# Two of a head's four casts on GpSimd instead of ScalarE, and its cluster rows sent with the first cast

## The chip, the core and the metric
The kernel runs on one core of a Trainium2 chip. Its engines work side by side, each through its own list of instructions in order: TensorE (PE; its weight loads are shown apart as PEld), VectorE (DVE), ScalarE (ACT), GpSimd (POOL) and SyncE (SP), which issues nearly all DMA transfers. The metric is the device time of one execution in microseconds (us), lower is better.

## The reference
The program is a chain of three stages; only the first is touched by the change. It is attention for 2 batches of 8 heads, sequence 768, head size 64, in which a query sees only the keys of its own cluster:

```
q_assign = argmax(einsum('bhsd,hcd->bhsc', q_n, c_n))     # 16 centroids a head
k_assign = argmax(einsum('bhsd,hcd->bhsc', k_n, c_n))
mask = q_assign[:, :, :, None] == k_assign[:, :, None, :]
scores = where(mask, q @ k.T / sqrt(64), -1e9)
attn = softmax(scores) @ v
```

Its output, 1536 rows of 512, goes through a mixture of 8 experts (each row to one expert, two matrix products with a ReLU), and then through a dense pair of products with a softplus between them.

## The kernel before, in words
**Tiles and order.** There are 16 heads, two to a pair p. A head has NT = 6 tiles of 128 queries, so the attention loop has 96 steps g = 6h + t. All engines' instructions are written out in this loop by hand, in program order; each engine works through its own in that order and waits by semaphores. In step g TensorE computes S, the scores, of tile g + 2, turns P of tile g (`P_T`, into the bank Tp), and does one piece of the product with v of the head before (`AV`). VectorE takes the row maximum `nm` of S, ScalarE the exponential P. The turned tile goes from Tp to PT in two halves: by VectorE and ScalarE, or both by ScalarE in steps listed in `busy`.

**Operands of S.** The products run in float32 with operands split into a rounded part and a rest. A head has four operand tiles, from a pool with two buffers of each: kA holds the rounded k in one half of the partitions and again in the other half, qA the rounded q and its rest, qB the rounded q, kB the rest of k. `prep_part(h, i)` makes them in four parts i = 0 to 3 at steps g = 6(h - 2) + 3 + i, so two heads ahead. Partitions 64 to 79 of qB and kB hold the one-hot cluster rows of queries and keys, by which the second product of S (L319) adds the mask. They are made for a pair at once in `mks[p]` (16 x 4 rows), and `put_mask(h)` copies them by four DMA transfers on SyncE's queue. L304, the first product of S, reads qA and kA; L319 reads qB and kB.

**Assignment of clusters.** `sims_mm`, `sims_T`, five small steps `sims_max` and `sims_back` make `mks[p]` during the pair before; for pairs from 3 on the third step, `eq` (L202), is on GpSimd, and the next, a maximum (L203), on VectorE. All transposes of this kind share one PSUM bank, misc.

**Other work in the loop.** `load_raw(p)` reloads q and k of a pair at step 12p - 25, once the old pair's are read. 16 pieces of the dense stage's weights come as 64-bit words (`cv_load`, 128 x 1024 x 8 bytes), are turned into float32 by ScalarE (`cvd`, L451) and VectorE (L453, L454, L459, L463), and are stored by SyncE (L469, w_rows).

The step's end, where the parts and the rows are called (before the change):

```
h2, i2 = divmod(g - 3, NT)
h2 += 2
if 2 <= h2 < NH and i2 < 4:
    prep_part(h2, i2)
    if i2 == 3 and h2 > 2:
        put_mask(h2)
```

Of the kernel before, what the change touches and what calls it, by code (L numbers as in the profile page):

```python
# [13 lines left out]
AF = mybir.ActivationFunctionType  # L14
ALU = mybir.AluOpType
# [17 lines left out]
def body(ctx, tc, qT, kT, vP, cen, mod, wg, bias, w1, w2, win, wout, out):  # L33
# [13 lines left out]
    pe, dve, act, pool, sp = nc.tensor, nc.vector, nc.scalar, nc.gpsimd, nc.sync  # L47
# [107 lines left out]
    def drain():  # L155
        while pend:
            for _ in pend.pop(0):
                pass

    def run(f, *a):  # L160

        drain()
        x = f(*a)
        if hasattr(x, "__next__"):
            next(x, None)
            pend.append(x)
# [101 lines left out]
    def prep_part(h, i):  # L268

        p, o = h // 2, 64 * (h % 2)  # L270
        if i == 0:
            spl[h] = tuple(p_sp.tile([128, S], F32R, tag=n, name=n) for n in ("qA", "kA", "qB", "kB"))
        qA, kA, qB, kB = spl[h]
        q_s, k_s = (r[o:o + 64] for r in raw[p])
        hi, lo = slice(o, o + 64), slice(64 - o, 128 - o)
        if i == 0:
            act.copy(kA[hi], k_s)
        elif i == 1:
            act.copy(kA[lo], k_s)
            dve.tensor_tensor(out=kB[0:64], in0=k_s, in1=kA[hi].bitcast(F32), op=ALU.subtract)  # L280
        elif i == 2:
            act.activation(out=qA[hi], in_=q_s, func=AF.Copy, scale=0.125)
        else:
            act.activation(out=qB[0:64], in_=q_s, func=AF.Copy, scale=0.125)
            dve.scalar_tensor_tensor(
                out=qA[lo], in0=q_s, scalar=0.125, in1=qA[hi].bitcast(F32), op0=ALU.mult, op1=ALU.subtract
            )

    def put_mask(h):
        p, i = h // 2, h % 2  # L290
        qA, kA, qB, kB = spl[h]
        for j, x in enumerate((qB, kB)):
            for a in range(2):
                o = 64 * j + 32 * a + 16 * i
                sp.dma_start(
                    out=x[64:80, a * HS:(a + 1) * HS].bitcast(F32), in_=mks[p][o:o + 16].bitcast(F32)
                )
# [11 lines left out]
    def S_mm(g):  # L309
        if g >= NH * NT:  # L310
            return
        if g not in S_t:
            S_part(g)
        h, t = divmod(g, NT)
        qA, kA, qB, kB = spl[h]
        ps = S_t[g]
        ts = slice(t * 128, t * 128 + 128)
        for i in range(2):
            pe.matmul(ps[:, i, :HS], qB[:80, ts], kB[:80, i * HS:(i + 1) * HS], start=False, stop=True)  # L319
        nm_t[g] = p_m.tile([128, 1], F32, tag="nm", name="nm", bufs=4)  # L320
        dve.tensor_reduce(out=nm_t[g], in_=ps[:, :, :HS], axis=AX.XY, op=ALU.max, negate=True)  # L321

    def S_exp(g):
        if g >= NH * NT:
            return
        h, t = divmod(g, NT)
        if t == 0:
            sums[h] = p_m.tile([128, NT], F32, tag="sums", name="sums", bufs=3)
        P_t[g] = p_P.tile([128, 2, HS], F32, tag="P", name="P")
        act.activation(  # L330
            out=P_t[g], in_=S_t.pop(g)[:, :, :HS], func=AF.Exp, bias=nm_t.pop(g), scale=1.0,
            accum_out=sums[h][:, t:t + 1],
        )

    def P_T(g):
        h, t = divmod(g, NT)
        if t == 0:
            PT[h] = p_PT.tile([128, NT, S], F32, tag="PT", name="PT")
        P = P_t.pop(g)
        for i in range(2):  # L340
            ps = ps_T.tile([128, 3, 128], F32, tag="t", name="Tp")
            for j in range(3):
                pe.transpose(ps[:, j, :], P[:, i, j * 128:(j + 1) * 128], ident)  # L343
            dst = PT[h][:, 3 * i:3 * i + 3, t * 128:(t + 1) * 128]
            if i == 0 and g not in busy:
                dve.tensor_copy(dst, ps)
            else:
                act.copy(dst, ps)  # L348
# [20 lines left out]
    def av_step(g):  # L369

        h, kt = divmod(g - NT - 1, NT)
        if kt == NT - 1:
            return
        AV(h, kt)
        if kt == NT - 2:
            AV(h, NT - 1)
            fin_av(h)
# [566 lines left out]
    with tc.manual_schedule():  # L944
# [147 lines left out]
        for g in range(NH * NT):  # L1092
            h, t = divmod(g, NT)
            if g > NT:
                av_step(g)
            S_mm(g + 2)
            P_T(g)
            for f, a in jobs.get(g, ()):
                if inspect.isgeneratorfunction(f):
                    run(f, *a)  # L1100
                else:
                    f(*a)
            S_exp(g + 2)
            drain()
            for f, a in after.get(g, ()):
                f(*a)
            h2, i2 = divmod(g - 3, NT)
            h2 += 2
            if 2 <= h2 < NH and i2 < 4:
                prep_part(h2, i2)  # L1110
                if i2 == 3 and h2 > 2:
                    put_mask(h2)
            if g == 8:
                put_mask(2)
# [450 lines left out]
        for c, y in enumerate((ys[NM - 1][1], ps_A.tile([128, 512], F32, tag="a", name="o"))):  # L1565
            cs = slice(c * 256, c * 256 + 256)
            for kt in range(16):
                gh, gl = gs[NM - 1, kt // 4]
                hi, lo = wts["out", kt // 2]
# [51 lines left out]
```

## Time and profile before

| what | value |
|---|---|
| median of 3 runs | 767.64 us (766.39 to 768.34) |
| the profiled execution, its own time | 767.36 us |
| its span in the profile | 765.6 us |
| busy in the span: TensorE, VectorE, ScalarE, GpSimd | 708.8, 450.0, 416.1, 128.5 us |

The span runs from the first to the last instruction in the profile; the execution's own time has 1.8 us more around it. Busy time is an average over stages that differ: attention ends near 297 us, the experts follow, and then the dense stage. "Granted clock" is the share of TensorE's full clock, of 2.4 GHz, that it was given in a stretch; the other level is 1.2 GHz. "Waited for" names what came last before an instruction could start.

### The profile page before, as it was taken

What the parts mean: (1) busy time and instruction counts of PE and PEld (TensorE: products, weight loads), DVE (VectorE), ACT (ScalarE), POOL (GpSimd) and SP (SyncE); (2) the same over time, 40 slices, a digit from 0 to 9 for tenths busy, and PEclk for the clock granted to TensorE, in tenths of its full rate; (3) what the DMA queues carried; (4) which work ended last, traced back from release to release, by engine and by line L of the source; (5) the groups of instructions that cost most, each with busy time, mean ns of one, the idle gap of its engine ahead of it and who ended that gap; (6) DMA issues with size and microseconds to landing.
All of it is one profiled execution on the core that took longest, in us unless ns stands there. A gap on an engine that the chain in (4) does not pass through costs nothing. (4 is left out here: it accounts for less than half of the span.)

```text
span 765.6 us, 11692 instructions
## 1 busy us (share of the span) xinstructions
PE 708.8 (93%) x4498; PEld 564.4 (74%) x4498; DVE 450.0 (59%) x668; ACT 416.1 (54%) x663; POOL 128.5 (17%) x144
## 2 busy tenths in 40 slices
PE   4997997899798999986999999998999999999998
PEld 2764654556455555874879888997998898999887
DVE  5895987789789975863446563677143233233220
ACT  3886987798779976343446562663323323323310
POOL 4200000000310103635452522252000000000000
PEclk9898999999989999996999999999999999999999
DMA  4314454544553625979967985500010000000000
GB/s 133 105 56 174 145 198 151 171 145 160 183 131 119 199 98 167 236 110 368 355 228 277 345 301 195 179 15 20 10 42 15 28 15 15 15 1 28 1 28 27
DMA packets 38683, 99.28 MB, mean 130 GB/s; under 512 B 8255, under 2 KB 15615, under 8 KB 36577
## 3 DMA queue, kind: packets, MB, share of 16 engines
q1 hardware_dynamic: 35888, 91.42, 36.3%
q0 software_dynamic: 2592, 6.69, 2.4%
q8 instruction: 36, 0.59, 0.3%
q10 hardware_dynamic: 144, 0.39, 0.2%
q14 instruction: 23, 0.18, 0.1%
HBM read 79.13 MB, written 18.28 MB: 127 GB/s over the span
## 5 line engine op out<-in xcount | busy, mean ns | idle before, releaser
L1500 DVE SCALAR_TENSOR_TENSOR sp<-g,sp 128x1024 f32<-128x1024 f32 x24 | 29.4, 1224 | 148.8 <-ACT sp L1499 148.8
L321 DVE TENSOR_REDUCE nm<-S 128x1 f32<-128x768 f32 x96 | 90.9, 948 | 34.3 <-PE S L319 34.0
L1489 PE MATMUL g<-xh,wh 128*128 128x256 f32 x384 | 108.7, 283 | 0.0
L1489 PE MATMUL g<-xh,wl 128*128 128x256 f32 x384 | 107.9, 281 | 0.0
L1489 PE MATMUL g<-xl,wh 128*128 128x256 f32 x384 | 107.9, 281 | 0.0
L1497 ACT ACTIVATE sp<-g 128x1024 f32<-128x1024 f32 x24 | 24.6, 1027 | 136.6 <-PE g L1489 126.7
L330 ACT ACTIVATE P<-S,nm 128x768 f32<-128x768 f32 x96 | 86.9, 905 | 18.9 <-DVE nm L321 16.2
L343 PE MATMUL Tp<-ident,P 128*128 128x128 f32 x576 | 85.6, 284 | 10.7 <-ACT PT L348 7.5
L343 PEld LDWEIGHTS Tp<-ident,P 128*128 128x128 f32 x576 | 68.7, 144 | 24.5 <-ACT PT L348 14.2
L355 PE MATMUL av<-PT,v 128*64 128x384 f32 x384 | 80.7, 517 | 0.0
L741 POOL TENSOR_TENSOR wl<-raw,wh 128x1024 fp32r<-128x1024 f32 x22 | 54.1, 2469 | 139.2 <-ACT wh L740 132.2
L741 DVE TENSOR_TENSOR wl<-raw,wh 128x1024 fp32r<-128x1024 f32 x50 | 65.1, 1343 | 14.5 <-ACT wh L740 14.5
L1489 PEld LDWEIGHTS g<-xl,wh 128*128 128x128 f32 x384 | 73.0, 190 | 0.5
L740 ACT CAST wh<-raw 128x1024 fp32r<-128x1024 f32 x69 | 68.9, 1050 | 8.0 <-DMA raw<-in_w 5.4
L1489 PEld LDWEIGHTS g<-xh,wh 128*128 128x128 f32 x384 | 72.8, 190 | 0.5
L348 ACT COPY PT<-Tp 128x384 f32<-128x384 f32 x144 | 64.0, 477 | 16.8 <-PE Tp L343 16.0
L1489 PEld LDWEIGHTS g<-xh,wl 128*128 128x128 f32 x384 | 73.0, 190 | 0.0
L1524 PE MATMUL o<-wh,gT 128*128 128x512 f32 x216 | 69.7, 394 | 0.0
L319 PE MATMUL S<-kB,qB 80*128 80x384 f32 x192 | 51.8, 353 | 18.0 <-DMA kB<-mk 16.1
L843 PE MATMUL y<-wh,hT 128*128 128x512 f32 x192 | 64.7, 408 | 0.0
L304 PEld LDWEIGHTS S<-kA,qA 128*128 128x128 f32 x192 | 29.7, 194 | 47.1 <-ACT PT L348 16.2
L304 PE MATMUL S<-kA,qA 128*128 128x384 f32 x192 | 60.2, 396 | 1.2 <-ACT P L330 0.9
(284 smaller groups left out, 1396.9 us busy)
## 6 DMA issues: line engine op xcount, KB each, us to landing
raw<-in_w SPq DMA_DIRECT2D x56, 512.0 KB, 7.6
words<-in_win SPq DMA_DIRECT2D x8, 1024.0 KB, 7.4
w_rows<-cvt SPq DMA_DIRECT2D x16, 512.0 KB, 3.0
words<-in_wout SPq DMA_DIRECT2D x8, 1024.0 KB, 5.7
whole<-in_w SPq DMA_DIRECT2D x16, 512.0 KB, 6.2
raw<-w_rows SPq DMA_DIRECT2D x16, 512.0 KB, 4.6
rawq<-in_qT SPq DMA_DIRECT2D x8, 384.0 KB, 3.4
v<-in_vP SPq DMA_DIRECT2D x8, 384.0 KB, 3.4
```

What stands on the lines that cost most here:

```text
L304: pe.matmul(ps[:, i, :HS], qA[:, t * 128:t * 128 + 128], kA[:, i * HS:(i + 1) * HS], start=True, stop=False)
L319: pe.matmul(ps[:, i, :HS], qB[:80, ts], kB[:80, i * HS:(i + 1) * HS], start=False, stop=True)
L321: dve.tensor_reduce(out=nm_t[g], in_=ps[:, :, :HS], axis=AX.XY, op=ALU.max, negate=True)
L330: act.activation(out=P_t[g], in_=S_t.pop(g)[:, :, :HS], func=AF.Exp, bias=nm_t.pop(g), scale=1.0, accum_out=sums[h][:, t:t + 1],)
L343: pe.transpose(ps[:, j, :], P[:, i, j * 128:(j + 1) * 128], ident)
L348: act.copy(dst, ps)
L355: pe.matmul(av_t[h][64 * a:64 * a + 64, :], vt[p][:, kt, 64 * i:64 * i + 64], PT[h][:, kt, a * HS:(a + 1) * HS], start=(kt == 0), stop=(kt ...
L740: cp(self.hi, self.raw)
L741: eng.tensor_tensor(out=self.lo, in0=self.raw, in1=self.hi.bitcast(F32), op=ALU.subtract)
L843: pe.matmul(u["y"][j], x, y, start=(kt == 0 and i == 0), stop=(kt == 7 and i == 2))
L1489: pe.matmul(o, a, b[:, kt, :], start=(n == 0 and f % 2 == 0), stop=(n == 11), skip_group_check=True)
L1524: pe.matmul(ys[u][j], x[:, a:a + 128], y, start=(kt == 0 and i == 0), stop=(kt == 15 and i == 2))
```

## The change
Two of a head's four casts, the second copy of the rounded k (part 1) and qB (part 3), go from ScalarE to GpSimd, where they stand in parts 0 and 2. The cluster rows are sent in part 0 instead of part 3, for heads from 3 on.

```diff
@@ -275,13 +275,13 @@
         if i == 0:
             act.copy(kA[hi], k_s)
+            pool.tensor_scalar(out=kA[lo], in0=k_s, scalar1=1.0, scalar2=1.0, op0=ALU.mult, op1=ALU.mult)
         elif i == 1:
-            act.copy(kA[lo], k_s)
             dve.tensor_tensor(out=kB[0:64], in0=k_s, in1=kA[hi].bitcast(F32), op=ALU.subtract)
         elif i == 2:
             act.activation(out=qA[hi], in_=q_s, func=AF.Copy, scale=0.125)
+            pool.tensor_scalar(out=qB[0:64], in0=q_s, scalar1=0.125, scalar2=1.0, op0=ALU.mult, op1=ALU.mult)
         else:
-            act.activation(out=qB[0:64], in_=q_s, func=AF.Copy, scale=0.125)
             dve.scalar_tensor_tensor(
                 out=qA[lo], in0=q_s, scalar=0.125, in1=qA[hi].bitcast(F32), op0=ALU.mult, op1=ALU.subtract
             )
@@ -1108,7 +1108,7 @@
             if 2 <= h2 < NH and i2 < 4:
                 prep_part(h2, i2)
-                if i2 == 3 and h2 > 2:
+                if i2 == 0 and h2 > 2:
                     put_mask(h2)
```

On SyncE, around the reload of pair 5 (steps 33 to 40), this stood before; the first two rows of L295 are the cluster rows of head 7:

```order
L469 DMA w_rows<-cvt 128x1024
L173 DMA rawq<-in_qT 128x768
L174 DMA rawk<-in_kT 128x768
L438 DMA words<-in_win 128x2048
L295 DMA qB<-mk 16x384 x2
L295 DMA kB<-mk 16x384 x2
L469 DMA w_rows<-cvt 128x1024
L438 DMA words<-in_win 128x2048
```

And this stands there now:

```order
L295 DMA qB<-mk 16x384 x2
L295 DMA kB<-mk 16x384 x2
L469 DMA w_rows<-cvt 128x1024
L173 DMA rawq<-in_qT 128x768
L174 DMA rawk<-in_kT 128x768
L438 DMA words<-in_win 128x2048
L469 DMA w_rows<-cvt 128x1024
L295 DMA qB<-mk 16x384 x2
L295 DMA kB<-mk 16x384 x2
L438 DMA words<-in_win 128x2048
```

Head 7's rows (the first pair of L295) stand ahead of the reload and of `words` now; head 8's (the second pair) stand between the store of the piece before and the next `words`.

On ScalarE, from the `cvd` of step 39 to head 8's cast of qA, before:

```order
L451 ACTIVATE cvd<-words 128x1024
L277 CAST kA<-rawk 64x768
L348 COPY PT<-Tp 128x3x128 x2
L330 ACTIVATE P,sums<-S,nm 128x768
L191 COPY sim<-misc 128x384
L279 CAST kA<-rawk 64x768
L362 COPY xTu<-av 128x384
L348 COPY PT<-Tp 128x3x128 x2
L330 ACTIVATE P,sums<-S,nm 128x768
L216 COPY simT<-misc 128x384
L282 ACTIVATE qA<-rawq 64x768
```

In the same place now one of the two casts of kA, L279, is gone:

```order
L451 ACTIVATE cvd<-words 128x1024
L277 CAST kA<-rawk 64x768
L348 COPY PT<-Tp 128x3x128 x2
L330 ACTIVATE P,sums<-S,nm 128x768
L191 COPY sim<-misc 128x384
L362 COPY xTu<-av 128x384
L348 COPY PT<-Tp 128x3x128 x2
L330 ACTIVATE P,sums<-S,nm 128x768
L216 COPY simT<-misc 128x384
L282 ACTIVATE qA<-rawq 64x768
```

On GpSimd, where before only the three `eq` of pairs 3 to 5 stood in a row, there are now the casts of heads 3 to 9 (L278 for kA, L283 for qB; these rows are heads 5 to 7):

```order
L278 TENSOR_SCALAR kA<-rawk 64x768
L202 TENSOR_TENSOR eq<-eq,desc 128x384
L283 TENSOR_SCALAR qB<-rawq 64x768
L278 TENSOR_SCALAR kA<-rawk 64x768
L283 TENSOR_SCALAR qB<-rawq 64x768
L278 TENSOR_SCALAR kA<-rawk 64x768
L202 TENSOR_TENSOR eq<-eq,desc 128x384
L283 TENSOR_SCALAR qB<-rawq 64x768
```

So `eq` of a pair stands behind the kA cast of an odd head, and that head's qB behind `eq`.

## Rows read from the trace of the kernel before

**Rows 1.** Table by stretches: busy us (instructions) per engine, granted clock, DMA share, GB/s.

```profile
core 0: us, PE busy (x) PEld busy (x) DVE busy (x) ACT busy (x) POOL busy (x), PEclk, DMA share, GB/s
24.00:297.00 273.00, 244.92 (x1462) 156.24 (x1460) 228.36 (x378) 228.39 (x443) 16.90 (x26) 0.97 0.44 148
...
136.00:141.00 5.00, 4.94 (x25) 2.49 (x25) 3.38 (x6) 4.33 (x8) 0.00 (x0) 0.67 0.25 102
```

**Rows 2.** Waits from 24 to 297 us: total us, times, longest.

```profile
PE S L319 <- DMA kB<-mk: 16.1, 5, 5.1
...
ACT P L330 <- DVE nm L321: 14.0, 19, 1.8
...
ACT cvd L451 <- DMA words<-in_win: 7.7, 2, 4.4
PE Tp L343 <- ACT PT L348: 7.5, 12, 1.3
...
ACT cvd L451 <- DMA words<-in_wout: 3.8, 1, 3.8
```

**Rows 3.** Timeline of TensorE: start, us, instruction [idle before, releaser].

```profile
63.09 0.98 PE L319 MATMUL S<-kB,qB 80*128 80x384 f32 x2 [4.35 <-DMA kB<-mk]
...
97.64 0.58 PE L319 MATMUL S<-kB,qB 80*128 80x384 f32 x2 [1.09 <-DMA kB<-mk]
...
136.06 0.98 PE L319 MATMUL S<-kB,qB 80*128 80x384 f32 x2 [5.11 <-DMA kB<-mk]
...
170.24 0.59 PE L319 MATMUL S<-kB,qB 80*128 80x384 f32 x2 [1.32 <-DMA kB<-mk]
...
207.95 1.01 PE L319 MATMUL S<-kB,qB 80*128 80x384 f32 x2 [4.25 <-DMA kB<-mk]
```

**Rows 4.** Timeline of SyncE's DMA queue at the reload of pair 5.

```profile
126.48 0.42 SPq L438 DMA_DIRECT2D words<-in_win  x1
127.00 1.24 SPq L295 DMA_DIRECT2D qB<-mk  x2
```

**Rows 5.** Timeline of VectorE and ScalarE around the wait at 136 us.

```profile
123.77 0.95 DVE L285 SCALAR_TENSOR_TENSOR qA<-rawq,qA 64x768 fp32r<-64x768 f32 x1
...
135.41 1.12 ACT L451 ACTIVATE cvd<-words 128x1024 f32<-128x1024 f32 x1 [4.37 <-DMA words<-in_win]
...
138.02 0.68 DVE L453 TENSOR_SCALAR cvd<-cvd 128x1024 f32<-128x1024 f32 x1
...
142.00 0.96 DVE L321 TENSOR_REDUCE nm<-S 128x1 f32<-128x768 f32 x1 [1.40 <-PE S L319]
...
145.09 0.56 DVE L387 TENSOR_TENSOR xb<-misc,rec 128x384 f32<-128x384 f32 x1
...
147.79 0.96 DVE L321 TENSOR_REDUCE nm<-S 128x1 f32<-128x768 f32 x1
```

**Rows 6.** The tile mk: its DMA transfers, from issue to landing.

```profile
DMA to landing us min/median/max: 1.8/2.4/8.6
```

**Rows 7.** Groups by line and form, 24 to 297 us: ScalarE's two casts (count, busy, mean ns).

```profile
L284 ACT ACTIVATE qB<-rawq 64x768 fp32r<-64x768 f32 x14 | 11.8, 844 | 0.2
...
L279 ACT CAST kA<-rawk 64x768 fp32r<-64x768 f32 x14 | 11.6, 831 | 0.3
```

**Rows 8.** The tile rawk: casts on GpSimd in the prologue, ns min/median/max.

```profile
L252 POOL TENSOR_SCALAR kA<-rawk x3: 830/832/836, 4.1 to 17.3; 64x768 fp32r<-64x768 f32 x3
```

**Rows 9.** Timeline of GpSimd: three of the `eq`.

```profile
111.02 1.86 POOL L202 TENSOR_TENSOR eq<-eq,desc 128x384 f32<-128x384 f32 x1 [30.84 <-DVE eq L201]
151.61 1.01 POOL L202 TENSOR_TENSOR eq<-eq,desc 128x384 f32<-128x384 f32 x1 [38.73 <-DVE eq L201]
...
225.63 1.00 POOL L202 TENSOR_TENSOR eq<-eq,desc 128x384 f32<-128x384 f32 x1 [14.16 <-DVE pm L613]
```

**Rows 10.** Timeline of VectorE beside them.

```profile
110.80 1.22 DVE L459 SCALAR_TENSOR_TENSOR cvt<-words,cvt 128x1024 int32<-128x1024 int32 x1
...
154.90 0.54 DVE L203 TENSOR_REDUCE m<-eq 128x24 f32<-128x384 f32 x1
...
225.65 1.01 DVE L613 TENSOR_SCALAR t<-t,pm 1x8 f32<-1x8 f32 x1
```

## The prediction, made before the changed kernel was run
> **What bounds the kernel now.** The change touches the attention stage alone, so I first read the table by stretches for it. From 24 to 297 us TensorE is busy 244.92 of 273 us, VectorE 228.36, ScalarE 228.39 and GpSimd 16.90 [rows 1]: TensorE is nearly full, two engines stand close behind it, one is empty. Next I read who waits for whom in the same stretch [rows 2]. TensorE waits 16.1 us in five pieces for the cluster rows in kB and 7.5 us in twelve pieces for ScalarE's copies of PT. ScalarE waits 7.7 + 3.8 us in three pieces for `words`, and 14.0 us in nineteen pieces for VectorE's row maximum `nm`.
>
> The five waits are those at the first tile of heads 3, 5, 7, 9 and 11: 4.35, 1.09, 5.11, 1.32 and 4.25 us [rows 3]. The order of the DMA queue shows why [rows 4]. For head 7 `words` go out at 126.48, after the reload of rawq and rawk, and the cluster rows only at 127.00. The reload had to wait for the last read of the old rawq, VectorE's qA, which runs from 123.77 for 0.95 us [rows 5]. By their shapes, pieces of 24 KB stand behind 1.8 MB. A mask transfer takes 2.4 us in the median and 8.6 at most [rows 6].
>
> The timeline of this event shows a second wait that the first one hides. ScalarE stands for 4.37 us until `words` land, at 135.41, and TensorE goes on at 136.06 [rows 3, 5]: the two transfers land 0.65 us apart. The three long waits are the three places where ScalarE waits for `words`; the two short ones have no such partner. After the long wait TensorE runs at a granted clock of 0.67 over 136 to 141 us [rows 1], that is partly at 1.2 GHz instead of 2.4; it had stood idle for 5.11 us before.
>
> **The change part by part.** *The rows earlier.* For the odd heads the four mask transfers now go out three tiles earlier, ahead of the pair's reload and `words`. They wait there for the last S of the head that used the buffer, which is in the same step, and SyncE then goes on. Seven tiles remain until the rows are read, where there were four. From head 3 to head 11, 48 tiles, it is 63.09 to 207.95 us [rows 3], 3.0 us a tile; seven are 21 us, and some 16 if a tile comes out a fifth faster, against at most 8.6. I expect all five waits for kB to go.
>
> What that is worth is not 16.1 us, because `words` are still late: the reload ahead of them still waits for qA, three steps before ScalarE's `cvd` reads them. I follow the event at 136 us. `words` still land at about 135.4, `cvd` ends at 136.53, and VectorE's L453 can start then, since the `nm` that ran ahead of it is already done. It started at 138.02 [rows 5], so 1.4 us are won. The next `nm` waited 1.40 us more for S at the low clock; that goes as well, 2.8 us. Then the chain through misc gives some back: the transposes for xb use the one misc bank, which is free only after ScalarE's simT, behind `cvd`, kA, two PT copies, P, sim, xTu, two PT copies and P, all dense from 135.41 on. I put simT's end at about 142.4, and so xb at 143.1 instead of 145.09; after that VectorE runs densely to the `nm` that began at 147.79 [rows 5], which comes out at about 145.8. That is 2.0 us for one event and 6 for the three. The store of cvt, which now no longer stands behind the mask transfers, goes out some us earlier and shares the queue with `words`; the next `words` go later, behind the next head's rows. I take 0.5 us off: 5.5. Bounds: 3 if the sharing delays every `words` by 1 us, 13.7 (4.35 + 5.11 + 4.25) if `words` were not late at all.
>
> The two short waits, 1.09 + 1.32 = 2.4 us, have nothing behind them but ScalarE and VectorE, both close to full. I take 2.0 (bounds 0 and 2.4).
>
> *Two casts less on ScalarE.* L279 and L284 take 831 and 844 ns, 14 times each [rows 7]: 23.4 us of ScalarE's 228.39. That time is on the path only where TensorE waits for ScalarE's PT: 7.5 us in twelve waits [rows 2]. A cast ahead of the wait can give back at most its 0.83 us, so the longest, 1.3 us, keeps some 0.5; I count 6.3 us as the most. VectorE is as full and ScalarE already waits 14.0 us for its `nm`, so I take 4 of it (bounds 0 and 6.3).
>
> *Two casts more on GpSimd.* Nothing but the engine's own queue holds them: kA waits for the last S that reads the old buffer, and qB follows at once. The same cast on GpSimd takes 832 ns at the kernel's start [rows 8], so a pair takes 1.7 us where the engine is busy 16.90 of 273 us. The first reader is S seven tiles later. Two costs are not covered by that. First, `eq` (L202) of every pair from 3 on stands in GpSimd's queue behind the new kA cast, and VectorE's next maximum (L203) waits for it. For pair 5 `eq` runs from 151.61 for 1.01 us and L203 begins at 154.90, 2.3 us after its end [rows 9, 10]; kA adds its 0.83 and waits for an S of the next step, which uses up most of that or a little more. Five pairs at up to 1 us: bounds 0 and 5, taken 1.5. Second, GpSimd and VectorE hinder each other. `eq` takes 1.01 us at 151.61 and 1.86 at 111.02, where VectorE's L459 with its two inputs runs from 110.80 for 1.22 us; and a VectorE operation on eight elements takes 1.01 us at 225.65, where `eq` runs from 225.63 for 1.00 [rows 9, 10]. It looks as if whichever comes second waits until the other's instruction is done. kA's cast mostly falls beside the row maximum, which also ran beside `eq` at 151.61 and did not slow it; qB's end meets whatever VectorE does next. I count 28 casts, a hindrance of 0 to 0.83 us each (0 to 23.2 us on VectorE), and take 1.5 in all, because GpSimd has no hurry and is as often the one that waits.
>
> The Trainium skill has a rule for this (SBUF — State Buffer, "Who interferes with whom"): GpSimd and VectorE share a port pair that is locked for a whole instruction, VectorE taking it in its two-port modes or with two inputs from SBUF. The two `eq` rows agree with it. By the rule at its worst the time would be the third rival's 780.6 us.
>
> **Sum.** 5.5 + 2.0 + 4.0 − 1.5 − 1.5 = 8.5 us won. What lies behind 297 us is issued in the same order and moves with it. The profiled execution took 767.36 us, 0.3 us from the median of the runs, so I predict **758.9 us**.
>
> **Rivals.**
> *First, `words` take the whole place of the mask.* They land 0.65 us before the mask does, so one may say that only 0.65 us of each long wait can go: 3 × 0.65 + 2.0 + 4.0 − 3.0 = 5.0 us, or 762.4; with nothing from the casts it is 766.4. For it: ScalarE waits in the same places. Against it: TensorE has one tile of work that needs no ScalarE, and the low clock after the wait goes if the gap is shorter. A next stage that waits for its weights, and so gives back part of the gain, would look the same from outside.
> *Second, more than I count.* All five waits go with little left of `words`, and the clock never falls: 13.7 + 2.4 + 4 − 3 = 17 us, 750. For it: the table shows TensorE at 0.67 after the wait. Against it: three steps are too few for `words` at the landing time seen here.
> *Third, slower: VectorE pays for the casts.* If GpSimd gets hold first and VectorE stands behind it, each cast moves from ScalarE to VectorE, which is just as full. The gains without contention are 5.5 + 2 + 4 − 1.5 = 10 us; over 28 casts that is the point from which it decides, 0.36 us of VectorE's time a cast. At the full 0.83 us it costs 23.2 and the kernel takes 780.6; at 0.5 it takes 771. For it: the 1.01 us on eight elements. Against it: a third of VectorE's time there is `nm`, beside which `eq` ran at 1.01.
> *Fourth, no change:* the mask is as late as before because the queue itself holds it back. Against it: the median of 2.4 us wherever nothing stands ahead.
>
> **How the numbers follow.** Forecast (755 to 762): 0.52. First rival (762 to 766): 0.20, of which 0.04 within 0.3%. Second (below 755): 0.12. Third (above 765): 0.11, of which 0.09 slower. Fourth: 0.05. A difference of 0.3% (2.3 us) is about what a measurement of this kernel can tell from none. So faster 0.80, same 0.11, slower 0.09. The range of 752 to 766 leaves out the far end of the second rival and most of the third, together under 0.2.
>
> **What would show it.** Right: no wait of S for kB or qB between 24 and 297 us; ScalarE still waiting 3 to 5 us for `words` three times; TensorE's gaps there 1.5 to 3 us instead of 4 to 5; ScalarE's busy time down by 23 us and GpSimd's up by about as much; fewer waits of Tp for ScalarE, more of P for `nm`. Wrong: VectorE's own instructions longer beside L278 or L283 (kB, L459, L453 above their usual length), L203 waiting for `eq`, or attention ending early and the expert stage no earlier.

## The result, and the profile after

The changed kernel takes 757.96 us in the median of seven runs (756.34 to 762.87), the kernel before, run beside it, 767.64 (764.09 to 771.98). The ratio is 0.9888 with a 95% interval of [0.9848, 0.9928]: faster by 0.7 to 1.5%, where 758.9 us was forecast. The profiled execution of the changed kernel took 757.96 us, its span 756.2.

The first part of its page (busy time, share of the span and instructions of each engine):

```profile
PE 706.8 (93%) x4498; PEld 565.8 (75%) x4498; DVE 455.2 (60%) x668; ACT 392.6 (52%) x635; POOL 157.1 (21%) x172
```

ScalarE lost 23.5 us of busy time against 416.1 before and GpSimd gained 28.6 against 128.5, as the move says. VectorE, which got no new work, is busy 5.2 us more than the 450.0 of before.

The waits from 24 to 290 us, of TensorE and then of ScalarE (us in total, times, longest):

```profile
PE Tp L343 <- ACT PT L348: 8.9, 11, 2.1
PE Tp L343 <- DVE PT L346: 4.3, 6, 1.2
PE S L304 <- ACT P L330: 2.7, 3, 1.0
...
ACT P L330 <- DVE nm L321: 31.9, 39, 1.8
ACT PT L348 <- PE Tp L343: 13.9, 20, 1.5
ACT cvd L451 <- DMA words<-in_win: 6.1, 2, 3.8
ACT cvd L451 <- DMA words<-in_wout: 3.9, 1, 3.9
```

The 16.1 us for kB of [rows 2] are gone: no line of TensorE names the cluster rows. The three waits for `words` stayed, 11.5 us before and 10.0 now. ScalarE waits 31.9 us for VectorE's `nm` where it waited 14.0: it is VectorE that ScalarE now runs up against.

The event that the prediction followed, once more (timeline of TensorE, ScalarE, VectorE and SyncE's DMA queue: start, us, instruction, and in brackets the idle time before it and what ended it):

```profile
125.96 1.69 SPq L295 DMA_DIRECT2D qB<-mk  x2
...
131.64 0.51 PE L319 MATMUL S<-kB,qB 80*128 80x384 f32 x2
131.87 1.12 ACT L451 ACTIVATE cvd<-words 128x1024 f32<-128x1024 f32 x1 [3.79 <-DMA words<-in_win]
133.02 0.69 DVE L453 TENSOR_SCALAR cvd<-cvd 128x1024 f32<-128x1024 f32 x1 [3.58 <-ACT cvd L451]
134.12 0.92 PE L343 MATMUL Tp<-ident,P 128*128 128x128 f32 x6 [1.97 <-ACT PT L348]
...
142.09 0.96 DVE L321 TENSOR_REDUCE nm<-S 128x1 f32<-128x768 f32 x1
```

S with kB runs at 131.64 without a wait; the rows sent at 125.96 are head 8's already. ScalarE still stands 3.79 us for `words`, and TensorE's gap is 1.97 us of waiting for PT instead of 5.11 for kB. The `nm` that began at 147.79 [rows 5] begins at 142.09. The table by stretches gives the clock behind this gap:

```profile
core 0: us, PE busy (x) PEld busy (x) DVE busy (x) ACT busy (x) POOL busy (x), PEclk, DMA share, GB/s
24.00:288.00 264.00, 243.25 (x1467) 157.96 (x1465) 234.78 (x380) 205.39 (x415) 47.23 (x70) 0.98 0.46 153
132.00:137.00 5.00, 2.32 (x14) 1.87 (x14) 3.91 (x7) 5.00 (x11) 0.00 (x0) 0.94 0.53 212
```

It is 0.94, where the five microseconds behind the wait showed 0.67 before [rows 1].

The table that follows comes from the timeline of ScalarE: the start of a tile's P (exp), of which there are 96, six to a head. The numbers are that start less the same start in the kernel before, in us. A long event (a reload with `words`) lies between tiles 17 and 19, 41 and 43, 65 and 67; a short one between 29 and 31, 53 and 55.

| tile | before, at | after | rows alone | casts alone | words early | words early, casts on ScalarE |
|---|---|---|---|---|---|---|
| 0 | 17.52 | +0.77 | +0.83 | +0.96 | +0.99 | +0.84 |
| 17 | 58.18 | +1.35 | +0.84 | +1.61 | +1.41 | +0.84 |
| 19 | 70.69 | −3.02 | −1.37 | +0.52 | −5.32 | −4.91 |
| 29 | 96.18 | −2.13 | −1.39 | +1.40 | −4.45 | −4.94 |
| 31 | 103.11 | −3.41 | −2.69 | +1.23 | −5.70 | −6.25 |
| 41 | 130.04 | −2.96 | −2.70 | +1.69 | −5.24 | −6.25 |
| 43 | 143.07 | −6.36 | −3.52 | +0.78 | −12.09 | −12.54 |
| 53 | 168.54 | −4.71 | −2.50 | +1.65 | −11.18 | −12.57 |
| 55 | 175.70 | −6.21 | −4.02 | +0.98 | −12.67 | −14.07 |
| 65 | 202.63 | −5.22 | −4.02 | +1.97 | −11.69 | −14.07 |
| 67 | 216.47 | −9.32 | −6.21 | +1.45 | −19.39 | −21.17 |
| 73 | 234.10 | −8.87 | −6.46 | +1.77 | −13.89 | −21.52 |
| 95 | 293.95 | −9.13 | −6.45 | +1.50 | −14.13 | −21.50 |

The column "after" wins 4.37 + 3.40 + 4.10 = 11.9 us at the long events and 1.28 + 1.50 = 2.8 at the short ones, and loses 5.5 us everywhere else, 0.77 of it before tile 0, where nothing was changed (other executions differ there by as much). From tile 95 to the end of the span it is 471.7 us before and 471.4 after, and 470.9 to 474.2 in the profiles of the experiments: that stretch varies by 3 us from profile to profile, so a profile's offset at tile 95 and a median can disagree by so much.

### The profile page after: what moved, and what is told of

It is laid out like the page before. It is cut to its first block, busy times and chain, and to the rows that moved or that the text cites. A ratio compares the mean times of both kernels' runs of the same rounds, so it can differ in the third digit from the quotient of the medians.

```text
span 756.2 us, 11743 instructions
## 1 busy us (share of the span) xinstructions
PE 706.8 (93%) x4498; PEld 565.8 (75%) x4498; DVE 455.2 (60%) x668; ACT 392.6 (52%) x635; POOL 157.1 (21%) x172
## 5 line engine op out<-in xcount | busy, mean ns | idle before, releaser
L818 PE MATMUL h<-xh,wh 128*128 128x256 f32 x192 | 55.1, 287 | 0.5 <-DVEq L1346 0.5
```

Of the source, the lines that this page charges most:

```text
L818: pe.matmul(o, a, b[:, kt, :], start=(n == 0 and f % 2 == 0), stop=(n == 11), skip_group_check=True)
```

## The experiments

The theories are F (the sum of the forecast), G (the casts on GpSimd cost VectorE what they free on ScalarE) and H (ScalarE is what bounds the kernel next). A ratio is always to the kernel before, run beside.

**Rows alone**, e1. The casts stay on ScalarE:

```diff
-                if i2 == 3 and h2 > 2:
+                if i2 == 0 and h2 > 2:
```

> The rows in part 0, all four casts on ScalarE. Theory F (the forecast's sum): the rows are worth 7.5 us and the casts 1.0, so this lands at about 760 us, ratio 0.990. Theory G (from the profile after: P starts 14.6 us earlier over the five waits and loses 4.7 us between them): the casts on GpSimd cost VectorE what they free on ScalarE, so this is as fast as the whole change or faster, 753 to 758 us, ratio 0.980 to 0.988, with VectorE's L453 and L454 back at 0.69 us. Theory H (ScalarE is the next bound once the rows are early): without the relief ScalarE takes the gain back, 762 to 766 us, and Tp waits for ScalarE's PT over 10 us between 24 us and the end of attention.

Measured: 762.43 us, ratio 0.9913 [0.9882, 0.9945]. Its waits from 24 to 290 us:

```profile
PE Tp L343 <- ACT PT L348: 16.0, 15, 3.6
...
ACT P L330 <- DVE nm L321: 12.6, 18, 1.8
ACT cvd L451 <- DMA words<-in_win: 8.9, 2, 5.4
...
ACT cvd L451 <- DMA words<-in_wout: 4.8, 1, 4.8
```

No wait for kB, but TensorE waits 16.0 us for PT behind a ScalarE that waits 13.7 us for `words`. By the table the rows alone win 2.21 + 0.82 + 2.19 = 5.2 us at the long events and 1.30 + 1.52 = 2.8 at the short ones. The ratio is F's (0.990), G's lies outside the interval, and H's sign, over 10 us of Tp waiting for PT, is there. What the casts add to the rows is known only roughly: the kernel before took 769.62 us beside this one and 767.64 beside the changed kernel, so it is 4.5 us by the medians, 1.9 by the ratios, whose intervals overlap, and 2.7 at tile 95.

**Casts alone**, e2. The changed kernel with `i2 == 3` put back.

> The two casts on GpSimd, the rows in part 3 as before. F: 1 us faster than before, 766 to 767 us, the five waits for kB still there. G: 1 to 5 us slower than before, 768 to 772 us, since VectorE's operations beside L278 and L283 grow as they did in the whole change (L453 and L454 together by 0.16 us each time). H: 2 to 4 us faster, because Tp's 7.5 us of waiting for ScalarE's PT go.

Measured: 768.56 us, ratio 0.9995 [0.9971, 1.0018]: no difference that can be told, against 769.62 beside it, so the time does not separate F's 1 us won from G's small loss. Waits of TensorE and ScalarE from 24 to 290 us, and a group of VectorE's (count, busy, mean ns):

```profile
PE S L319 <- DMA kB<-mk: 14.2, 5, 4.5
...
ACT P L330 <- DVE nm L321: 30.6, 40, 1.8
...
L454 DVE TENSOR_SCALAR cvt<-cvd 128x1024 int32<-128x1024 int32 x16 | 12.6, 790 | 0.6
```

The freed ScalarE time shortens the five events by 3.4 us together, and 3.9 us are lost between them (1.50 at tile 95, plus 3.36, less the 0.96 of tile 0). ScalarE's wait for `nm` is 30.6 us and L454 takes 790 ns instead of 694, with the rows still late: both belong to the casts and not to the rows, as G says.

**No reads**, e3. GpSimd fills the second copy of kA, and qB, with a memset instead of casting, so two of a head's casts are left out (kA's line is shown, qB's is changed in the same way):

```diff
-            pool.tensor_scalar(out=kA[lo], in0=k_s, scalar1=1.0, scalar2=1.0, op0=ALU.mult, op1=ALU.mult)
+            pool.memset(kA[lo].bitcast(F32), 0.0)
```

> The whole change, but GpSimd fills the two tiles with a constant instead of reading q and k: the two casts are left out of the computation, the instructions that write their tiles stay in place and order. G (GpSimd's reads of SBUF hold VectorE up): L453, L454 and the operations with two inputs go back to their lengths of before, and the kernel is 2 to 4 us faster than the whole change, 754 to 756 us. F, and any theory in which the loss between the waits is only VectorE's fullness and not the contention: no more than 1.5 us faster than the whole change.

Measured: 757.54 us, ratio 0.9871 [0.9836, 0.9906], the same as the whole change within its interval. Three groups of VectorE's in the changed kernel from 24 to 290 us (count, busy, mean ns):

```profile
L454 DVE TENSOR_SCALAR cvt<-cvd 128x1024 int32<-128x1024 int32 x16 | 12.8, 801 | 0.6
L453 DVE TENSOR_SCALAR cvd<-cvd 128x1024 f32<-128x1024 f32 x16 | 11.9, 741 | 10.8 <-ACT cvd L451 10.7
...
L430 DVE TENSOR_TENSOR lacc<-lacc,ltmp 128x48 f32<-128x48 f32 x10 | 3.4, 336 | 0.3
```

and in the kernel without reads:

```profile
L454 DVE TENSOR_SCALAR cvt<-cvd 128x1024 int32<-128x1024 int32 x16 | 12.1, 756 | 0.6
L453 DVE TENSOR_SCALAR cvd<-cvd 128x1024 f32<-128x1024 f32 x16 | 11.2, 700 | 9.5 <-ACT cvd L451 9.5
L430 DVE TENSOR_TENSOR lacc<-lacc,ltmp 128x48 f32<-128x48 f32 x10 | 2.2, 215 | 0.3
```

With rows alone they take 694, 686 and 208 ns. So L430, which adds two tiles, is free again once GpSimd only writes; L454, with one input, is hindered by the writes too, by about half as much. The profile is 3.1 us ahead of the changed kernel's at tile 95 (281.71 us), and its last 474.2 us take 2.8 more than there: the medians can't tell the two apart, and the reads' share in time stays at 0 to 3 us. Between the events this profile loses 2.73 us (its tile 0 is 0.88 us late, the events win 15.85, and tile 95 is 12.24 ahead of before), rows alone lose 0.76 there and the changed kernel 4.75. So only half of the 4.0 us that the casts cost there goes with the reads, although VectorE's busy time is then 451.2 us, within 1.3 us of rows alone. What the other half is was not shown.

The Trainium skill (SBUF — State Buffer, "Who interferes with whom") says that a VectorE instruction with two inputs in SBUF collides with a GpSimd instruction that reads SBUF and not with one that only writes, and that one in a two-port mode, which a tensor_scalar can enter, shuts GpSimd out or is shut out for a whole instruction. The two sets of rows agree: 336 against 215 ns for L430, 801 and 756 for L454.

**Words early**, e4. The changed kernel, and `words` loaded one tile sooner:

```diff
-            job(g0 - 4, cv_load, j)
+            job(g0 - 5, cv_load, j)
```

> The whole change, and each piece of the 64-bit words is called for one step earlier, so that it stands ahead of a pair's reload instead of behind it. If the words' landing is what is left of the three long waits (forecast, main point), ScalarE's 10 us of waiting for words go and with them TensorE's gaps of 1.1, 2.0 and 2.1 us before Tp and the low clock behind the third: 4 to 7 us faster than the whole change, 751 to 754 us. If VectorE is the bound there anyway, the words' wait goes and the time stays within 1.5 us of the whole change.

Measured: 753.95 us, ratio 0.9816 [0.9787, 0.9844]. No wait for `words` is left. That is 4.0 us faster than the whole change by the medians and 5.5 by the ratios, as forecast if `words` were what was left. The table shows 21 us won at tile 67 and 5.5 of them lost again by tile 73. The timeline of that place (GpSimd, VectorE, ScalarE):

```profile
213.90 0.83 POOL L278 TENSOR_SCALAR kA<-rawk 64x768 fp32r<-64x768 f32 x1 [12.48 <-DMA token_list<-tokid,ridx]
214.82 1.00 POOL L202 TENSOR_TENSOR eq<-eq,desc 128x384 f32<-128x384 f32 x1
215.85 0.55 DVE L203 TENSOR_REDUCE m<-eq 128x24 f32<-128x384 f32 x1 [2.99 <-POOL eq L202]
...
219.20 0.92 DVE L321 TENSOR_REDUCE nm<-S 128x1 f32<-128x768 f32 x1
...
220.21 0.90 ACT L330 ACTIVATE P<-S,nm 128x768 f32<-128x768 f32 x1 [4.12 <-DVE pm L613]
```

Head 13's kA cast waits until the six scatters of the token list have landed, `eq` stands behind it in GpSimd's queue, VectorE's L203 waits for `eq`, and P for the row maximum that stands behind L203 and ends at 220.12 (the bracket names the small `pm` right behind it). In the changed kernel the cast stands behind the same scatters; there it began at 217.14, and the profile puts its wait down to TensorE's Tp.

**Casts doubled**, e5. Each GpSimd cast of the changed kernel is written a second time (kA's is shown; a set is 28 casts):

```diff
             pool.tensor_scalar(out=kA[lo], in0=k_s, scalar1=1.0, scalar2=1.0, op0=ALU.mult, op1=ALU.mult)
+            pool.tensor_scalar(out=kA[lo], in0=k_s, scalar1=1.0, scalar2=1.0, op0=ALU.mult, op1=ALU.mult)
```

> The changed kernel with each of the two casts of a head written twice in a row on GpSimd (the second writes the same values again). Three theories. F, the forecast's sum: a set of 26 casts costs VectorE 1.5 us on the path and the queue of GpSimd 1.5 us, so a second set gives about 758.0 + 1.5 to 3 = 759.5 to 761. G: the casts cost VectorE what was measured between the events, 4.0 us for a set (after against rows alone, and casts alone against before), and a second set costs about as much again: 761 to 763, with the 1024-wide VectorE operations (L453, L454) longer again than 741 and 801 ns. H, ScalarE is the next bound and GpSimd's work is hidden: 758, no change.

Measured: 766.33 us, ratio 0.9964 [0.9942, 0.9986]: slower than the changed kernel by 8.4 us by the medians and 5.8 by the ratios, more than any theory said, and the direction is G's. The page and two groups of VectorE's (here L456 and L432 are what is L454 and L430 elsewhere):

```profile
PE 712.0 (93%) x4498; PEld 568.7 (74%) x4498; DVE 461.3 (60%) x668; ACT 392.8 (51%) x635; POOL 186.6 (24%) x200
...
L456 DVE TENSOR_SCALAR cvt<-cvd 128x1024 int32<-128x1024 int32 x16 | 13.0, 812 | 0.6
...
L432 DVE TENSOR_TENSOR lacc<-lacc,ltmp 128x48 f32<-128x48 f32 x10 | 6.7, 668 | 0.3
```

VectorE's busy time for the same 668 instructions is 449.9 us without casts on GpSimd (rows alone), 455.2 with one set and 461.3 with two. That L454 would grow again was wrong (812 against 801 ns); of the second set's 6.1 us L430 took the largest part (6.7 us in all against 3.4). This profile's execution took 770.09 us, 3.8 above the median. In it, against the changed kernel, 9.1 us more are lost between the events, 3.8 of them between tiles 67 and 73, where GpSimd's kA cast now waits 11.3 us for the scatters, as in e4; and the events win 3.2 us less.

**Words early, casts on ScalarE**, e6. Before, with the two one-line edits of e1 and e4.

> The rows sent with the first cast and the words loaded one tile earlier, with both casts on ScalarE as before: the kernel with early words less the casts. It asks what the casts are worth once neither the mask nor the words end the wait. F: as much as with the words late, 762.4 - 758.0 = 4.5 us, so 754.0 + 4.5 = 758.5. G: the 6.7 us that the casts won at the three long events were won because ScalarE came to its words sooner; with the words there this is gone and the 4.0 us that VectorE pays remain, so the casts are worth nothing or less: 750 to 754. H, ScalarE bound: 760 or more.

Measured: 746.02 us, ratio 0.9698 [0.9672, 0.9723], far below both kernels. With `words` early the casts on GpSimd cost 753.95 − 746.02 = 7.9 us (the kernel before took 769.6 beside the one and 769.5 beside the other), more than G's best case for this run. TensorE's waits from 24 to 290 us, and VectorE's group:

```profile
PE Tp L343 <- ACT PT L348: 7.7, 13, 1.3
PE Tp L343 <- DVE PT L346: 2.9, 3, 1.2
...
L454 DVE TENSOR_SCALAR cvt<-cvd 128x1024 int32<-128x1024 int32 x16 | 11.1, 694 | 0.6
```

ScalarE, with 22 us more to do, waits no more for `words`, and 14.0 us for VectorE's `nm` where it waits 31.6 in e4; TensorE's waits of Tp for both engines are 10.6 us against 13.2 in the changed kernel. H falls. The last two columns of the table say where the 7.4 us at tile 95 are: 5.9 from tile 67 to 73, 3.4 between the other events, 0.15 before tile 0, and 2.1 the other way at the events, where the casts still help ScalarE.

**One cast back**, e7. Words early, with head 13's kA cast alone on ScalarE:

```diff
+            if h == 13:
+                act.copy(kA[lo], k_s)
+            else:
```

> The kernel with early words, with one of its 28 casts put back on ScalarE: kA of head 13, which the program lets wait for the landing of the six scatters of the token list and which stood 12.5 us at 213.9 with the eq of the third event behind it. If that wait is on the path, the 5.5 us that this kernel loses between tiles 67 and 73 come back in large part: 749 to 751. Rival: another wait of the same place (VectorE's late row maxima, ScalarE with one cast more) takes it over: 753 to 755.

Measured: 748.30 us, ratio 0.9723 [0.9699, 0.9746]: one cast of 28 is worth 5.6 us. Its timeline of GpSimd and VectorE at that place:

```profile
207.65 1.01 POOL L202 TENSOR_TENSOR eq<-eq,desc 128x384 f32<-128x384 f32 x1 [7.01 <-DVE pm L616]
...
211.90 0.54 DVE L203 TENSOR_REDUCE m<-eq 128x24 f32<-128x384 f32 x1
```

`eq` runs 7 us sooner and L203 waits for nothing. That the wait of e4 was on the path is shown; from tile 67 to 73 this kernel loses 2.5 us where e4 loses 5.5.

**Half the casts**, e8. Words early, kA's cast on ScalarE in all heads, qB's on GpSimd.

> The kernel with early words, with kA's cast back on ScalarE in all heads and only qB's on GpSimd. G: half of VectorE's 4.0 us comes back (2 us) and the wait for the six scatters no longer stands ahead of the eq (up to 5.5 us), against half of ScalarE's relief lost: 748 to 752. F: half of ScalarE's relief lost, 2.2 us, and only the wait of 5.5 us or a part of it against it: 751 to 756. H: ScalarE bound again, above 756.

Measured: 748.64 us, ratio 0.9721 [0.9697, 0.9744]. It lies with e7 and 2.6 us above e6, with intervals that overlap; at tile 95 it is 1.7 us behind e6. VectorE is busy 452.3 us, about halfway from 449.7 in e6 to 454.0 in e4. The direction is G's once more.

**Words early alone**, e9. Before, with the edit of e4 only: rows late, casts on ScalarE.

> The kernel before with the words loaded one tile earlier and nothing else: the rows are sent with the fourth cast, the casts stay on ScalarE. It completes the square of rows and words. If the long waits were the mask's rows behind a megabyte of words that leaves half a microsecond ahead of them, a words load that leaves some 3 us sooner takes away a part of the mask's wait and of its own: the 16.1 us of waits for kB's rows fall to 8 or less and the time to 755 to 760. If the rows were late by their own issue, whatever is ahead of them, the waits stay at 13 or more and hide the sooner words: 765 to 768.

Measured: 762.26 us, ratio 0.9907 [0.9873, 0.9942], between the two cases. TensorE's wait for the rows is

```profile
PE S L319 <- DMA kB<-mk: 12.7, 4, 6.3
```

in four places instead of five: at tile 43 this kernel is 11.2 us ahead of before, and between 53 and 55, then 67 and 73, it loses 5.9 and 6.2 us. At the three long events it wins 5.8, 6.3 and 7.1 us, the same as e6 with both edits: there the rows were late only because they stood behind the late `words`. The two long waits that remain are 4.9 us at 162.61, where the reload and `words` go out at 152 to 153 us, just ahead of the rows (153.99), and 6.3 us at 220.78, for rows that went out at 207.15 to 209.6, while the six scatters (198.54 to 207.1) were under way; that the one and the other held them is likely and not shown. So the two edits want each other: each alone is worth 0.9%, both together 3.0%.

**Words two tiles early**, e10. As e6 with `g0 - 6`.

> The rows with the first cast, both casts on ScalarE, and the words loaded two tiles earlier than before instead of one. No wait for words is left in the kernel with one tile, so the theory says no further gain: 745 to 747.5. Rivals: the words still hold ScalarE for less than the view shows and 2 us or more come off (744 or less); or the sooner megabyte collides with other loads and stores and costs it (749 or more).

Measured: 744.38 us (743.79 to 746.34), ratio 0.9682 [0.9647, 0.9716], against 746.02 (745.00 to 749.36) and 0.9698 [0.9672, 0.9723] for one tile. The intervals overlap widely, and at tile 95 the two are 0.6 us apart, as they were at tile 0 already. No further gain can be told.

## Why the forecast came out right

The sum was 8.5 us; the medians say 9.7 and the profiles 9.4. Its terms, against the rows and casts measured apart (e1 less before, and after less e1):

| term | forecast | measured |
|---|---|---|
| three long waits, by the rows | 5.5 | 5.2 |
| two short waits, by the rows | 2.0 | 2.8 |
| ScalarE relieved | 4.0 | 6.6, all at the long events |
| `eq` and L203 behind the casts | −1.5 | 0 |
| VectorE and GpSimd hinder each other | −1.5 | −4.0 between the events, half of it without GpSimd's reads |

*The long waits.* That `words` keep most of the place of the mask was right. The size was right in the sum and not event by event: 2.2, 0.8 and 2.2 us with rows alone, and the followed event is the one of 0.8. There `words` took 9.93 us from issue to `cvd` where they had taken 8.93 (8.39 and 9.53 against 8.25 and 8.45 at the other two), about the 1 us that the lower bound of 3 put down to sharing the queue; what they shared it with was not tested. In the changed kernel ScalarE waits there 2.30, 3.79 and 3.91 us, and TensorE's gaps are 1.13, 1.97 and 2.12 us. For the followed `nm` 2.0 us were forecast and 5.7 came (147.79 to 142.09), since the events ahead of it and the casts are in it too.

*ScalarE relieved* was sized too small, and came out above its bound of 6.3 (6.6, if each of the twelve waits is counted up to 0.83 us). I had looked for it at TensorE's twelve short waits for PT, and those did not shrink: 7.5 us in twelve before, 8.9 in eleven after. It came at the long events: at the second, P of tile 43 follows that of tile 41 by 9.63 us after and by 12.21 with rows alone. There `words` arrive 1.6 us sooner after P of tile 41, and the work from `cvd` to P is 1.0 us shorter, about one cast. Once `words` are early the casts win only 2.1 us at all events (e4 against e6): the relief was worth that much because ScalarE was late through another wait. Why `words` land sooner with the casts gone was not settled; they are issued 0.5 us sooner, and the rest is in the transfer (from issue to `cvd` 8.80 against 9.93 us).

*The eq queue* cost nothing here: no wait of L203 for `eq` is in the changed kernel. The mechanism is right, and shows in e4 with 3.0 us of wait and 5.5 us lost, by a price that the prediction put at nothing: the wait of one kA cast for the scatters ahead of it.

*Contention* was sized too small by 2.5 us, within its bounds, if all that the casts cost between the events is put down to it: 3.9 us with rows late (e2), 4.0 with rows early (after less e1), 3.4 in e4 beside the scatters' wait, and 5.3 more with a second set (e5, also beside it). That GpSimd's work slows VectorE is shown by the lengths; of the 4.0 us, e3 gives 2.0 to the reads and leaves 2.0 open. The rate is 4.0 / 28 = 0.14 us a cast, well under the 0.36 at which the third rival would have decided. That it was listed among the signs of a wrong forecast was too strict: L453 and L454 did grow, and the kernel was faster all the same.

The errors have both signs: +0.5 for the rows' two terms, +2.6, +1.5 and −2.5 make 2.1 us, against which the profile sets 0.8 at tile 0 and 0.8 between the events of e1. Part of the agreement is luck.

*The rivals.* The first gives 762.4, where the whole change took 757.96: it left the long waits 2.0 us where 5.2 were won. (That rows alone take 762.43 is chance, since the first counts 4.0 us for the casts.) The second, 750, needed `words` not to be late, which e4 makes true: 753.95, and 746.02 without the casts (e6). The third is real in sign, with 4.0 us or less of its 23.2. The fourth falls: no wait for the rows is left.

## What to carry to other kernels

When two transfers land within a microsecond of each other, removing one wait shows the other: plan both edits, since rows and `words` gave 0.9% each and 3.0% together. Work moved to an idle engine is free only if that engine shares nothing with the one that is next to be late, and what it is worth changes with the wait around it: the same casts won 2 to 4.5 us while `words` were late and cost 7.9 us when they were not. Before moving work, read what it will wait for on the new engine, and what stands behind it there; one cast of 28 was worth 5.6 us.

## What the runs showed of the hardware

The collision is not a slowdown spread over both instructions. In the changed kernel, on GpSimd and VectorE:

```profile
76.15 0.96 DVE L321 TENSOR_REDUCE nm<-S 128x1 f32<-128x768 f32 x1
76.84 1.00 POOL L202 TENSOR_TENSOR eq<-eq,desc 128x384 f32<-128x384 f32 x1
77.29 1.10 DVE L453 TENSOR_SCALAR cvd<-cvd 128x1024 f32<-128x1024 f32 x1 [0.19 <-ACT cvd L451]
77.93 1.16 POOL L283 TENSOR_SCALAR qB<-rawq 64x768 fp32r<-64x768 f32 x1
78.43 1.21 DVE L454 TENSOR_SCALAR cvt<-cvd 128x1024 int32<-128x1024 int32 x1
```

L453 ends 0.55 us after `eq` does (78.39 and 77.84), and L454 0.55 us after qB's cast (79.64 and 79.09), though each had begun 0.55 to 0.66 us before that end, and takes 0.69 us undisturbed. It looks as if each stands, nearly whole, behind the one that came first, and the other engine's next one behind it in turn: qB's cast took 1.16 us instead of 0.83. GpSimd pays as well: its 28 casts take 1.07 us each in the mean, 6.6 us more in all than at 0.83. Not every VectorE instruction pays: the row maximum takes 944 to 948 ns in the mean in every kernel here, and the two-input L459 and L463, which are longer, 1.21 us with one set of casts on GpSimd as without, and 1.24 to 1.27 with two.
